# The first projection's weight split and the last value sum change place at the start of attention

## The chip, the cores and the metric

The kernel runs on one core of a Trainium2 chip. The metric is the device time of one execution in microseconds; a kernel's time is the median of its runs.

## What is computed

Two layers are applied to x (2048 x 1024, float32); each is an attention block and a spectral block with residuals:

```python
qkv = (lambda x, *d: x.transpose(*d))((x @ wqkv).reshape(B, S, 3, H, Dh), 2, 0, 3, 1, 4)
q, k, v = qkv[0], qkv[1], qkv[2]
scores = jnp.einsum("bhqd,bhkd->bhqk", q, k) * (Dh ** -0.5)
p = _softmax(scores, axis=-1)
o = jnp.einsum("bhqk,bhkd->bhqd", p, v)
return (lambda x, *d: x.transpose(*d))(o, 0, 2, 1, 3).reshape(B, S, D) @ wo
...
x = x + _A_ref(_layernorm(x, axis=-1), A_wqkv, A_wo)
x = x + _B_ref(_layernorm(x, axis=-1), B_w_r, B_w_i)
x = x + _A_ref(_layernorm(x, axis=-1), A_wqkv, A_wo)
x = x + _B_ref(_layernorm(x, axis=-1), B_w_r, B_w_i)
```

There are 32 heads of 32 columns. `_B_ref` multiplies the two-dimensional Fourier transform of its input by a weight and transforms back; the change does not touch it.

## The kernel before, in words

`attention` (called once per layer) handles the heads in 8 groups g of 4 heads, 128 columns each. Every float32 operand of a projection is split in a high and a low float16 half by `split` (ACT makes the high half, L167, VectorE the low one, L168); a projection is then three products: high by high, high by low, low by high.

**Weights.** `Weights.prep(ph)` is a generator for one phase ph: ("k", g), ("q", g) or ("v", g). It loads the weights in pieces of 256 KB from the SP queue (L251) into one of three staging buffers `wst`, then splits each piece into `wqk` (two buffers) or `wv`. In layer 0 it also takes the largest magnitude of each piece on VectorE (L259, tile `fw`).

**Projections.** `qk_chunk(ph, c)` makes 512 rows of keys or queries: 24 matmuls (L338) into one PSUM bank, then a split of the result and its square (L342). `v_tiles(ph, t)` makes one value sum, 256 rows for two groups: 48 matmuls (L382) into one bank, evacuated by two ACT instructions (L386). `bank()` gives these sums a bank: while the list `both` is not empty, o and x in turn; afterwards x alone, which exists once.

**Prologue.** The normalised input is written to `big` in float16 halves. Then the keys and queries of group 0 (four chunks each) and eight value sums are made, the latter as the list `vk`; three of them stand behind the loop over c, in bank o, x and o. Ahead of these three, `norms()` twice takes the largest squared norm of keys and of queries: matmuls with a matrix of ones (L355) and a maximum on VectorE (L357, `mqk`). `mkbias` makes the softmax bias from both on POOL: an all-reduce over the partitions (L363, `mall`) and three small instructions, the last at L368.

**Units.** After the prologue the order on TensorE and ACT is the order of the code, written by hand (`tc.manual_schedule`); the other engines are ordered by the scheduling layer. A unit is a group g, a chunk c of 512 queries and a tile kt of 128 keys. `S` makes its scores: 12 matmuls (L563) into two of the three double banks `psS`, then two exponentials on ACT (L567) into `p` (eight buffers). `PV` multiplies by the values (L573, bank o), two units at a time, at every even unit. `add` sums the exponentials on VectorE (L584 for the second unit of a chunk, L586 else). After every odd unit, the generator `filler` supplies eight matmuls of the next groups' projections: its first phase is ("k", 1), whose sums use bank x. It first calls `prep` for that phase, so the split stands behind the exponentials of the first two units.

The lines of the code in these steps are below; those numbers are the profile's.

Of the kernel before, what the change touches and what calls it, by code (L numbers as in the profile page):

```python
# [164 lines left out]
def split(nc, hi, lo, src, scale):  # L165

    nc.scalar.activation(hi, src, AF.Copy, scale=scale)  # L167
    nc.vector.scalar_tensor_tensor(lo, src, scale, hi, op0=ALU.mult, op1=ALU.subtract)  # L168


def run(g):
    for _ in g:
        pass
# [53 lines left out]
class Weights:  # L227
# [5 lines left out]
    def prep(self, ph):  # L233
        nc, ap, wp = self.nc, self.ap, self.wp
        kind, g = ph
        if kind == "v":
            w = self.W[ph] = ap.wvp.tile([128, 2, 8, 256], F16, name="wv")
            sl = [(w[:, 0, 4 * j:4 * j + 4, 128 * i:128 * i + 128], w[:, 1, 4 * j:4 * j + 4, 128 * i:128 * i + 128],
                   wp[g + i, 2, :, 512 * j:512 * j + 512]) for i in range(2) for j in range(2)]
        else:  # L240
            w = self.W[ph] = ap.wqp.tile([128, 2, 8, 128], F16, name="wqk")
            sl = [(w[:, 0, 4 * j:4 * j + 4], w[:, 1, 4 * j:4 * j + 4],
                   wp[g, 0 if kind == "q" else 1, :, 512 * j:512 * j + 512]) for j in range(2)]
        st = []

        def load():
            if len(st) < len(sl):
                pool, tag = ap.stages[self.n % len(ap.stages)] if self.flag is not None and ph in PH0 else (ap.sgp, "wst")
                self.n += 1
                s = pool.tile([128, 4, 128], F32, name="wst", tag=tag)  # L250
                nc.sync.dma_start(s, sl[len(st)][2].rearrange("p (d c) -> p d c", c=128))  # L251
                st.append(s)
        for _ in range(4 if self.flag is not None and ph in PH0 else 3):
            load()
        yield
        for i, (h, l, _) in enumerate(sl):
            split(nc, h, l, st[i], SW)
            if self.flag is not None:
                nc.vector.tensor_reduce(self.flag.pop(), st[i], axis=AX.XY, op=ALU.max, apply_absolute_value=True)  # L259
            load()  # L260
            yield
# [6 lines left out]
def attention(nc, tc, layer, ap, xin, yd, wts, wo, cst, dram, flags):  # L268
# [4 lines left out]
    W, prep = wts.W, wts.prep  # L273
# [50 lines left out]
    def qk_chunk(ph, c):  # L324
        kind, g = ph
        w = W[ph]
        if c == 0:
            if kind == "k":
                K[g] = ap.k[g % 3]
            else:  # L330
                Q[g] = qp.tile([128, 2, 2048], F16, name="Q") if g % 2 else ap.q
            p_, n_ = (qp, "Q") if ph == ("q", 0) else (sq, "sq")
            nrm[ph] = p_.tile([128, 4, 512], BF16, name="sq", tag=n_)
        t = (K if kind == "k" else Q)[g][:, :, c * 512:c * 512 + 512]
        ps = bank()
        for d in range(8):
            for i, (a, b) in enumerate(((w[:, 0, d], xh[c][:, d]), (w[:, 0, d], xl[c][:, d]), (w[:, 1, d], xh[c][:, d]))):
                nc.tensor.matmul(ps, a, b, start=d == 0 and i == 0, stop=d == 7 and i == 2)  # L338
                if d < 7 or i < 2:
                    yield  # L340
        split(nc, t[:, 0], t[:, 1], ps, SQ / (SX * SW))
        (nc.gpsimd if both else nc.vector).tensor_tensor(nrm[ph][:, c], t[:, 0], t[:, 0], op=ALU.mult)  # L342
        if c == 3:
            left_norms.append(ph)
        yield
# [24 lines left out]
    def v_tiles(ph, t2):  # L370

        _, g = ph
        w = W[ph]
        if t2 == 0:
            V[g], V[g + 1] = ap.v[g % 3], ap.v[(g + 1) % 3]
        ps = bank().rearrange("p (t n) -> p t n", n=256)
        for j in range(2):
            c, o = t2 // 2, (t2 % 2) * 256 + j * 128
            for d in range(8):
                a, b = xh[c][:, d, o:o + 128], xl[c][:, d, o:o + 128]  # L380
                for i, (l, r) in enumerate(((a, w[:, 0, d]), (a, w[:, 1, d]), (b, w[:, 0, d]))):
                    nc.tensor.matmul(ps[:, j], l, r, start=d == 0 and i == 0, stop=d == 7 and i == 2)  # L382
                    if (3 * d + i) % 2 and (j, d, i) != (1, 7, 2):
                        yield
        for i in range(2):
            nc.scalar.activation(V[g + i][:, 2 * t2:2 * t2 + 2], ps[:, :, 128 * i:128 * i + 128], AF.Copy, scale=1.0 / (SX * SW))  # L386
        yield
# [4 lines left out]
    phases = [ph for g in range(NG - 1) for ph in beside[g]]  # L392

    def sums(ph):
        return 8 if ph[0] == "v" else 4

    def filler():
        run(prep(phases[0]))
        for i, ph in enumerate(phases):
            nxt = prep(phases[i + 1]) if i + 1 < len(phases) else iter(())  # L400
            for n in range(sums(ph)):
                yield from (v_tiles if ph[0] == "v" else qk_chunk)(ph, n)
                for _ in range(1 + (n > 0)):
                    next(nxt, None)
            run(nxt)
# [95 lines left out]
    def wo_rest(t):  # L501
        p = psS.tile([128, 2, 512], F32, name="s")
        nc.vector.bn_aggr(mvs[:, 2 * t:2 * t + 2], wo_last(t // 4, t % 4, p, wo_dst[t], wo_dst[t], True))
# [19 lines left out]
    vk = [v_tiles(PH0[0], t) for t in range(8)]  # L523
# [16 lines left out]
    for c in range(NCH):  # L540
        for i, ph in enumerate(PH0[1:]):
            if c < 2:
                ln(8 + 4 * c + 2 * i, 2)
            run(qk_chunk(ph, c))
        if c == 3:
            norms()
            norms()
        else:
            run(vk.pop(0))
    for v in vk:  # L550
        run(v)
    both.clear()
# [4 lines left out]
    def S(g, c, kt):  # L557

        s = [psS.tile([128, 2, 512], F32, name="s") for _ in range(2)]
        for i, (a, b) in enumerate(((0, 0), (0, 1), (1, 0))):  # L560
            for h in range(4):
                r = slice(32 * h, 32 * h + 32)
                nc.tensor.matmul(s[h // 2][:, h % 2], K[g][r, a, kt * 128:kt * 128 + 128],  # L563
                                 Q[g][r, b, c * 512:c * 512 + 512], start=i == 0, stop=i == 2)
        for hf in range(2):
            p = P[g, c, kt, hf] = pp.tile([128, 2, 512], F32, name="p")
            nc.scalar.activation(p, s[hf], AF.Exp, bias=bias[g], scale=SCALE / (SQ * SQ))  # L567
# [65 lines left out]
    with tc.manual_schedule(engines={mybir.EngineType.PE, mybir.EngineType.Activation}):  # L633
        for g in range(NG):
            todo = sum(sums(ph) for ph in beside.get(g, []))
            sl = slots(fill, todo, 22 if g == NG - 2 else 32, 24)
            wsl = slots(wof, 4, 10, 21)
            for u in range(NCH * NKT):
                c, kt = divmod(u, NKT)
                S(g, c, kt)  # L640
                if kt % 2 == 0:
                    for w in pend:
                        PV(*w)
                    late = pend
                    pend = []
                for w in late[:1]:
                    add(*w)
                    if w[2] == NKT - 1:
                        fin(*w[:2])
                        done = [w[:2]]  # L650
                late = late[1:]
                if kt == 5 and done:
                    out(*done.pop())
                pend.append((g, c, kt))
                if kt % 2 == 0:
                    continue
                if todo:
                    todo = next(sl)
                elif g == NG - 2:
                    if left:  # L660
                        run(lwo)
                        left = 0
                    if next(wsl, None) is not None and u == NCH * NKT - 1:
                        run(wsl)
                elif g == NG - 1:
                    for _ in range(share[u // 2]):
                        next(wof)
                    if u // 2 in rests:
                        wo_rest(rests[u // 2])
                if g == NG - 2 and todo < 4:  # L670
                    for _ in range(2):
                        if left > (8 if todo == 3 else 0):
                            next(lwo, None)
                            left -= 1
        for w in pend:
            PV(*w)
        for w in late + pend:
            add(*w)
        run(wof)
# [559 lines left out]
```

## Time and profile before

| what | value |
|---|---|
| median of 3 runs | 3857.41 us (3855.62 to 3857.58) |
| profiled execution | 3855.25 us |
| its span, first to last instruction | 3853.3 us |
| instructions in the span | 79584 |
| PE busy | 3720.5 us (97%) |
| DVE (VectorE) busy | 3165.8 us (82%) |
| ACT (ScalarE) busy | 2898.3 us (75%) |
| POOL (GpSimd) busy | 303.0 us (8%) |
| mean granted TensorE clock | 0.990 |

PE is the matmul side of TensorE, PEld its weight loads, SPq the queue from which SyncE issues DMAs. A row of the timeline gives the start in microseconds from the span's start, the length, the engine, the line, the operation, written tile <- read tiles, the shape and how many instructions were merged into the row; in brackets stands how long the engine was idle before and what ended that. "Granted clock" is the share of full TensorE clock that the chip allowed in a stretch.

### The profile page before, as it was taken

The numbers are of one execution on the slowest core, as the hardware profiler recorded it, in microseconds if no ns is written. First come the engines' busy times: TensorE is split into PE (matmuls) and PEld (weight loads), VectorE is DVE, ScalarE is ACT, GpSimd is POOL, SyncE is SP. The second block draws the span as 40 slices with busy tenths as digits, with TensorE's granted clock in tenths as the row PEclk, the third lists the DMA queues.
The fourth block names the chain that finished last, engine by engine and source line by source line (L and its number), as shares of the span: only waits on it lengthen the run. The fifth ranks groups of instructions, "written<-read, shape, count | busy, mean of one in ns | idle before, by whom it ended". The sixth has DMA issues, their size and how long they took to land.

```text
span 3853.3 us, 79584 instructions
## 1 busy us (share of the span) xinstructions
PE 3720.5 (97%) x32951; PEld 1640.1 (43%) x32951; DVE 3165.8 (82%) x3869; ACT 2898.3 (75%) x3567; POOL 303.0 (8%) x386
## 2 busy tenths in 40 slices
PE   6999999999999999999989999999999999999998
PEld 4322433342234233378853334333423432333788
DVE  6699899889998988866666998899899889889554
ACT  4678887888788866667756888888888888666585
POOL 1000000000000000004320000000000000000143
PEclk9999999999999999999999999999999999999999
DMA  8000000000000221243270000000000002112433
GB/s 206 15 12 23 12 12 18 18 12 18 12 26 7 73 71 64 80 149 124 63 175 15 18 18 13 12 18 23 10 18 12 23 12 91 53 64 72 150 99 104
DMA packets 165573, 194.07 MB, mean 50 GB/s; under 512 B 74960, under 2 KB 120656, under 8 KB 164176
## 3 DMA queue, kind: packets, MB, share of 16 engines
q1 hardware_dynamic: 164912, 188.82, 15.9%
q8 instruction: 260, 4.26, 0.5%
q14 instruction: 113, 0.93, 0.1%
q10 hardware_dynamic: 288, 0.07, 0.0%
HBM read 123.83 MB, written 48.23 MB: 45 GB/s over the span
## 4 chain that ended last, share of the span: by engine, by line
PE 73%; DVE 12%; issue 8%; ACT 3%; DMA 2%; POOL 2%; SPq 0%; DVEq 0%; POOLq 0%; ACTq 0%
PE o L573 19%; PE s L563 16%; PE x L338 12%; PE x L382 7%; PE x L441 6%; DVE R L586 4%; PE s L441 2%; PE ps L861 2%; PE ps L801 2%; ACT p L567 1%; PE s L592 1%; PE ps L792 1%; DMA wst<-in_wp 1%; PE ps L976 1%; PE ps L930 1%
## 5 line engine op out<-in xcount | busy, mean ns | idle before, releaser
L567 ACT ACTIVATE p<-s,bias 128x1024 f32<-128x1024 f32 x2048 | 2167.8, 1111 | 553.5 <-PE s L563 542.6
L586 DVE TENSOR_TENSOR R<-R,p 128x1024 f32<-128x1024 f32 x1792 | 2085.4, 1219 | 111.2 <-ACT p L567 107.8
L573 PE MATMUL o<-p,R 128*32 128x512 f32 x8192 | 985.0, 598 | 0.0
L338 PE MATMUL x<-big,wqk 128*128 128x512 f16 x2880 | 682.7, 383 | 21.1 <-DVE Q L168 6.5
L563 PEld LDWEIGHTS <-R 32*128 32x128 f16 x12288 | 231.6, 92 | 760.3 <-issue 644.6
L338 PEld LDWEIGHTS <-wqk 128*128 128x128 f16 x3072 | 277.6, 98 | 458.5 <-issue 165.4
L563 PE MATMUL s<-R 32*128 32x512 f16 x6144 | 430.9, 378 | 10.6 <-ACT p L567 8.9
L573 PEld LDWEIGHTS o<-p,R 128*32 128x32 f32 x8192 | 213.7, 109 | 523.8 <-issue 523.8
L563 PE MATMUL s<-Q,R 32*128 32x512 f16 x6144 | 425.4, 378 | 7.5 <-DVE R L482 5.5
L382 PEld LDWEIGHTS <-big 128*128 128x128 f16 x3072 | 293.1, 99 | 144.3 <-issue 66.2
L382 PE MATMUL x<-wv,big 128*128 128x256 f16 x2688 | 320.5, 275 | 35.0 <-DMA big<-hl 35.0
L584 DVE SCALAR_TENSOR_TENSOR R<-p 128x1024 f32<-128x1024 f32 x128 | 153.8, 1203 | 198.9 <-ACT p L567 198.6
L441 PE MATMUL x<-big 128*128 128x512 f16 x1050 | 241.6, 380 | 0.0
L363 POOL PARTITION_ALL_REDUCE mall<-mqk x16 | 41.8, 2612 | 2325.5 <-DVE mqk L357 2313.9
L441 PEld LDWEIGHTS <-big 128*128 128x128 f16 x1344 | 124.3, 98 | 180.5 <-issue 42.7
L909 DVE TENSOR_TENSOR H<-G,H 128x512 f16<-128x512 f32 (+1 forms) x68 | 46.3, 680 | 113.1 <-ACT H L908 112.9
L861 PE MATMUL ps<-cbi,H 128*128 128x256 f16 (+1 forms) x792 | 100.5, 275 | 7.9 <-ACT H L908 6.2
L854 ACT COPY U<-ps 64x256 f32<-64x256 f32 (+1 forms) x272 | 97.0, 357 | 11.6 <-PE ps L861 6.4
L854 ACT COPY B<-ps 64x256 f32<-64x256 f32 (+1 forms) x272 | 97.0, 356 | 7.0 <-PE ps L861 2.8
L861 PE MATMUL ps<-cb,big 128*128 128x256 f16 x780 | 97.6, 275 | 0.0
L167 ACT ACTIVATE R<-x 128x512 f16<-128x512 f32 x88 | 52.6, 598 | 54.8 <-PE x L338 54.7
L806 DVE TENSOR_TENSOR big<-ps,big 128x512 f16<-128x512 f32 x64 | 44.4, 694 | 50.4 <-ACT big L805 50.3
(428 smaller groups left out, 2967.7 us busy)
## 6 DMA issues: line engine op xcount, KB each, us to landing
wst<-in_wp SPq DMA_DIRECT2D x96, 256.0 KB, 3.0
R<-y SPq DMA_DIRECT2D x32, 512.0 KB, 5.4
w<-in_w SPq DMA_DIRECT2D x60, 256.0 KB, 2.7
od<-ohl SPq DMA_DIRECT2D x56, 256.0 KB, 2.4
big<-od SPq DMA_DIRECT2D x16, 896.0 KB, 7.0
y<-R SPq DMA_DIRECT2D x20, 512.0 KB, 2.6
R<-in_x SPq DMA_DIRECT2D x16, 512.0 KB, 5.6
wst<-in_wo SPq DMA_DIRECT2D x32, 256.0 KB, 3.0
```

Of the source, the lines that this page charges most:

```text
L167: nc.scalar.activation(hi, src, AF.Copy, scale=scale)
L338: nc.tensor.matmul(ps, a, b, start=d == 0 and i == 0, stop=d == 7 and i == 2)
L382: nc.tensor.matmul(ps[:, j], l, r, start=d == 0 and i == 0, stop=d == 7 and i == 2)
L441: nc.tensor.matmul(p, a, b, start=start and d == ds[0] and i == 0, stop=stop and d == ds[-1] and i == 2)
L563: nc.tensor.matmul(s[h // 2][:, h % 2], K[g][r, a, kt * 128:kt * 128 + 128], Q[g][r, b, c * 512:c * 512 + 512], start=i == 0, stop=i == 2)
L567: nc.scalar.activation(p, s[hf], AF.Exp, bias=bias[g], scale=SCALE / (SQ * SQ))
L573: nc.tensor.matmul(O[g, c][32 * h:32 * h + 32], V[g][:, kt, 32 * h:32 * h + 32], P[g, c, kt, h // 2][:, h % 2], start=kt == 0, stop=kt == ...
L584: nc.vector.scalar_tensor_tensor(acc[hf], P[g, c, 0, hf], 1e-34, p, op0=ALU.add, op1=ALU.add)
L586: nc.vector.tensor_add(acc[hf], acc[hf], p)
L801: nc.tensor.matmul(pa[:, j], tt[:, j], mm[:, g], start=True, stop=True)
L854: nc.scalar.copy(ov[64 * r:64 * r + 64, a0:a0 + m, x], tl[64 * x:64 * x + 64, :m, r])
L861: nc.tensor.matmul(out, l, r, start=k == 0, stop=k == len(mm_) - 1)
```

## The change

```diff
@@ -395,7 +395,6 @@
         return 8 if ph[0] == "v" else 4
 
     def filler():
-        run(prep(phases[0]))
         for i, ph in enumerate(phases):
             nxt = prep(phases[i + 1]) if i + 1 < len(phases) else iter(())
             for n in range(sums(ph)):
@@ -547,6 +546,8 @@
             norms()
         else:
             run(vk.pop(0))
+    run(prep(phases[0]))
+    last_v = vk.pop()
     for v in vk:
         run(v)
     both.clear()
@@ -638,6 +639,8 @@
             for u in range(NCH * NKT):
                 c, kt = divmod(u, NKT)
                 S(g, c, kt)
+                if g == u == 0:
+                    run(last_v)
                 if kt % 2 == 0:
                     for w in pend:
                         PV(*w)
```

`phases[0]` is ("k", 1). Its preparation is moved from the start of `filler` to a place ahead of the last three value sums. The last of the eight value sums is taken out of the list and run between the scores of unit 0 and those of unit 1; `both` is empty by then, so it takes bank x. Both layers are changed alike. Between the second and the third piece of the diff lines count one higher in the changed kernel (L563 is L564 there, L567 is L568).

In the orders below the first place is ScalarE in layer 0, from the evacuation of the last key chunk to the first units. `R<-o 128x512` and `R<-x 128x512` are the high halves of key and query chunks, `R<-o 128x256` and `R<-x 128x256` evacuations of value sums, `p<-s,bias` the exponentials, `wqk<-wst` the split's high halves. Before:

```order
L167 ACTIVATE R<-o 128x512
L167 ACTIVATE R<-x 128x512
L386 ACTIVATE R<-o 128x256 x2
L386 ACTIVATE R<-x 128x256 x2
L386 ACTIVATE R<-o 128x256 x2
L567 ACTIVATE p<-s,bias 128x1024 x4
L167 ACTIVATE wqk<-wst 128x512 x2
L567 ACTIVATE p<-s,bias 128x1024 x8
```

And in the changed kernel:

```order
L167 ACTIVATE R<-o 128x512
L167 ACTIVATE wqk<-wst 128x512 x2
L167 ACTIVATE R<-x 128x512
L386 ACTIVATE R<-o 128x256 x2
L386 ACTIVATE R<-x 128x256 x2
L568 ACTIVATE p<-s,bias 128x1024 x2
L386 ACTIVATE R<-x 128x256 x2
L568 ACTIVATE p<-s,bias 128x1024 x10
```

The two high halves moved from behind the fourth exponential to ahead of the last query chunk, and the last value sum's evacuation from ahead of the first exponential to behind the second.

The second place is VectorE in layer 0 at the same point. `wqk<-wst,wqk` are the split's low halves, `fw<-wst` the magnitudes of staged weights, `mqk<-s` the maxima for the bias, `R<-p` and `R<-R,p` the sums of exponentials. Before:

```order
L168 SCALAR_TENSOR_TENSOR R<-o,R 128x512 x2
L357 TENSOR_REDUCE mqk<-s 128x1
L168 SCALAR_TENSOR_TENSOR R<-x,R 128x512
L357 TENSOR_REDUCE mqk<-s 128x1
L584 SCALAR_TENSOR_TENSOR R<-p 128x1024 x2
L168 SCALAR_TENSOR_TENSOR wqk<-wst,wqk 128x512 x2
L259 TENSOR_REDUCE fw<-wst 128x1 x2
L586 TENSOR_TENSOR R<-R,p 128x1024 x8
```

And in the changed kernel:

```order
L168 SCALAR_TENSOR_TENSOR R<-o,R 128x512 x2
L168 SCALAR_TENSOR_TENSOR wqk<-wst,wqk 128x512 x2
L259 TENSOR_REDUCE fw<-wst 128x1 x2
L357 TENSOR_REDUCE mqk<-s 128x1
L168 SCALAR_TENSOR_TENSOR R<-x,R 128x512
L357 TENSOR_REDUCE mqk<-s 128x1
L585 SCALAR_TENSOR_TENSOR R<-p 128x1024 x2
L587 TENSOR_TENSOR R<-R,p 128x1024 x8
```

The low halves and two magnitudes moved ahead of both maxima. In layer 1 the low halves move in the same way, and there are no magnitudes. The two magnitudes belong to pieces that are loaded into the staging buffers which the split has freed.

The third place is TensorE in layer 0, where the second of the three late value sums (bank x) ends. Before, the third sum (bank o) follows it directly:

```order
L382 MATMUL x<-wv,big 128x256
L382 LDWEIGHTS big
L382 MATMUL x<-wv,big 128x256
L382 LDWEIGHTS big
L382 MATMUL o<-wv,big 128x256
```

In the changed kernel unit 0's twelve score matmuls follow it, and where these end stand:

```order
L564 LDWEIGHTS R
L564 MATMUL s<-R 128x512
L382 LDWEIGHTS big
L382 MATMUL x<-wv,big 128x256
L382 LDWEIGHTS big
```

The last sum's 48 matmuls moved behind unit 0's scores and into bank x. They are followed by unit 1's scores and the first eight matmuls of ("k", 1). POOL and the SP queue keep their order.

## The prediction, made before the result was known

> **What bounds the kernel now.** The first view is the chain of work that ended last, by engine:
>
> ```profile
> PE 73%; DVE 12%; issue 8%; ACT 3%; DMA 2%; POOL 2%; SPq 0%; DVEq 0%; POOLq 0%; ACTq 0%
> ```
>
> TensorE holds most of that chain, so the question at any place is when TensorE stands still. The change touches one place in each of the two layers: the passage from the prologue's value sums to the first score units. The second view is therefore the table by stretches (columns: length, busy time of PE, weight loads, DVE, ACT and POOL, then the granted TensorE clock), cut at that passage:
>
> ```profile
> 118.25:123.59 5.34, 5.34 (x50) 4.61 (x48) 0.00 (x0) 0.66 (x2) 1.05 (x3) 1.00 0.00 0
> 123.59:133.09 9.50, 5.18 (x33) 1.39 (x32) 3.56 (x4) 5.82 (x8) 0.00 (x0) 0.82 0.14 45
> 133.09:143.51 10.42, 10.42 (x98) 3.13 (x98) 8.94 (x9) 8.03 (x8) 0.00 (x0) 1.00 0.03 11
> 2046.81:2057.96 11.15, 6.95 (x46) 1.70 (x45) 3.57 (x4) 5.82 (x8) 0.00 (x0) 0.69 0.15 47
> ```
>
> During the last value sum (118.25 to 123.59) TensorE is busy throughout at clock 1.00. In the 9.50 us behind it, it works 5.18 us at a granted clock of 0.82, then it is full again. Layer 1 shows the same passage as 11.15 us, with 6.95 us of work at 0.69. The third view, the timeline, says what stands in it (layer 0, one engine's group per row: start, length):
>
> ```profile
> 113.67 0.37 POOL L363 PARTITION_ALL_REDUCE mall<-mqk  x1 [5.61 <-issue]
> 118.25 5.40 PE L382 MATMUL o<-wv,big 128*128 128x256 f16 x48
> 118.45 0.66 ACT L386 ACTIVATE R<-x 128x256 f32<-128x256 f32 x2 [4.58 <-PE x L382]
> 121.81 0.27 POOL L368 TENSOR_SCALAR bias<-bpr 128x1 f32<-128x1 f32 x1
> 123.59 1.03 PE L563 MATMUL s<-R 32*128 32x512 f16 x14
> 124.50 4.13 ACT L567 ACTIVATE p<-s,bias 128x1024 f32<-128x1024 f32 x4
> 125.67 0.82 PE L563 MATMUL s<-R 32*128 32x512 f16 x10 [1.04 <-ACT p L567]
> 127.66 2.36 DVE L584 SCALAR_TENSOR_TENSOR R<-p 128x1024 f32<-128x1024 f32 x2 [18.44 <-ACT p L567]
> 128.50 1.16 ACT L167 ACTIVATE wqk<-wst 128x512 f16<-128x512 f32 x2
> 129.94 1.29 DVE L168 SCALAR_TENSOR_TENSOR wqk<-wst,wqk 128x512 f16<-128x512 f32 x2
> 130.65 0.93 SPq L251 DMA_DIRECT2D wst<-in_wp  x2
> 130.68 2.49 PE L338 MATMUL x<-big,wqk 128*128 128x512 f16 x6 [0.56 <-DVE wqk L168]
> 133.10 0.82 PE L563 MATMUL s<-R 32*128 32x512 f16 x12
> 133.42 1.33 DVE L259 TENSOR_REDUCE fw<-wst 128x1 f32<-128x512 f32 x2 [2.20 <-DMA wst<-in_wp]
> 133.85 1.92 PE L573 MATMUL o<-p,R 128*32 128x512 f32 x16
> 133.96 2.12 ACT L567 ACTIVATE p<-s,bias 128x1024 f32<-128x1024 f32 x2 [4.29 <-PE s L563]
> ```
>
> Read it as a relay. Scores of unit 0 at 123.59; unit 1's second half has no free score bank (three banks, two per unit) until the first exponential ends, so it starts at 125.67. ACT makes four exponentials, 124.50 to 128.63, and only then rounds the weights of the first projection (128.50, x2). VectorE makes their low halves at 129.94. TensorE's eight projection matmuls wait for both: two begin behind the high half, six at 130.68. Unit 2's scores come at 133.10, its first exponential at 133.96. The bias that every exponential needs was ready at 121.81 + 0.27 = 122.08, so today it delays nothing.
>
> **The change, part by part.** No instruction is added or removed; in each layer 48 matmuls, 4 ACT and 2 or 4 VectorE instructions change place, and the last sum takes bank x instead of o.
>
> *The split moved ahead.* It now stands behind the evacuation of the last key sum, since it overwrites the buffer of the key weights. The rows around its new place:
>
> ```profile
> 101.17 0.60 ACT L167 ACTIVATE R<-o 128x512 f16<-128x512 f32 x1 [4.52 <-PE o L338]
> 101.80 0.69 DVE L168 SCALAR_TENSOR_TENSOR R<-o,R 128x512 f16<-128x512 f32 x1 [9.73 <-ACT R L167]
> 101.84 1.04 POOL L342 TENSOR_TENSOR sq<-R 128x512 bf16<-128x512 f16 x1 [9.38 <-ACT R L167]
> 106.77 0.69 DVE L357 TENSOR_REDUCE mqk<-s 128x1 f32<-128x512 f32 x1 [4.28 <-PE s L355]
> 107.38 0.68 DVE L168 SCALAR_TENSOR_TENSOR R<-x,R 128x512 f16<-128x512 f32 x1
> 108.53 0.69 DVE L357 TENSOR_REDUCE mqk<-s 128x1 f32<-128x512 f32 x1 [0.47 <-PE s L355]
> ```
>
> ACT rounds from 101.77 to 102.93 (2 x 0.58 from 1.16); its next duty is the query sum whose low half follows at 107.38, so it is hidden. VectorE makes the low halves from about 102.5 to 103.8 (1.29), also in idle time. In layer 0 two reductions of the *next* staged weights follow on VectorE, ahead of the two maxima from which the bias is made. They wait for DMAs that the freed stage buffers release. Before, the issue at 130.65 let the reduction run at 133.42, 2.77 us later. The first low half now ends at 103.15, so the reductions run from about 105.97 to 107.3 (1.33 for both). The first maximum then starts at 107.3 instead of 106.77, the other sum's low half at 108.0, the second maximum at 108.7 instead of 108.53: at most 0.17 us on the bias, 122.25 at worst. The all-reduce row starts 4.4 us behind that maximum's end, so perhaps nothing; I take 122.14 for the first exponential and keep 122.3 for the range. Layer 1 has no such reductions; its maxima don't move. The SP queue keeps its order: only those two weight DMAs go out earlier, about 103.2 and 103.8.
>
> [...]
>
> *The last value sum between units 0 and 1, layer 0.* How close groups follow each other is read in the steady loop:
>
> ```profile
> 152.09 1.90 PE L338 MATMUL x<-big,wqk 128*128 128x512 f16 x8
> 152.19 2.12 ACT L567 ACTIVATE p<-s,bias 128x1024 f32<-128x1024 f32 x2 [0.49 <-PE s L563]
> 153.92 0.82 PE L563 MATMUL s<-R 32*128 32x512 f16 x12
> 154.67 1.92 PE L573 MATMUL o<-p,R 128*32 128x512 f32 x16
> 154.78 2.12 ACT L567 ACTIVATE p<-s,bias 128x1024 f32<-128x1024 f32 x2 [0.47 <-PE s L563]
> ```
>
> Eight projection matmuls to the next scores take 153.92 - 152.09 = 1.83 us; scores to what follows 0.75; the exponential starts 0.86 behind its scores. Then:
> - Unit 0's scores start at 118.36 (when the last sum did, plus the 0.11 seen at 123.59). Their exponentials start at 122.14 and take 4.13 / 2 = 2.07: 124.21.
> - The last sum starts behind them and behind the evacuation of bank x (118.45 + 0.66 = 119.11): about 119.2, for 5.23, to 124.45. So TensorE works while the bias is made; that is the cover.
> - ACT evacuates it from 124.68 (0.2 behind the next group's start, as at 118.45) to 125.34; it is free by then.
> - Unit 1's scores: 124.48 to 125.23. Their banks are free since the first exponential's end, 123.2.
> - The projection's eight matmuls need bank x, thus 125.34: start 125.40. Weights and low halves lie ready since 104.
> - Unit 2's scores: 125.40 + 1.83 = 127.23; exponential 128.09. Unit 1's end at 127.5, so nothing waits.
>
> Against 133.96 this is **5.87 us** earlier. What goes is the wait for the bank, the wait for the weights and the half-speed matmuls (six in 2.49 us against eight in 1.90).
>
> *Layer 1*, where the bias is late relative to TensorE:
>
> ```profile
> 2037.22 0.37 POOL L363 PARTITION_ALL_REDUCE mall<-mqk  x1 [5.94 <-issue]
> 2041.48 5.40 PE L382 MATMUL o<-wv,big 128*128 128x256 f16 x48
> 2045.53 0.27 POOL L368 TENSOR_SCALAR bias<-bpr 128x1 f32<-128x1 f32 x1
> 2056.57 1.46 PE L563 MATMUL s<-R 32*128 32x512 f16 x12
> 2057.96 1.92 PE L573 MATMUL o<-p,R 128*32 128x512 f32 x16
> 2058.07 2.12 ACT L567 ACTIVATE p<-s,bias 128x1024 f32<-128x1024 f32 x2 [5.18 <-PE s L563]
> ```
>
> Unit 0's scores at 2041.59; last sum 2042.42 to 2047.65. Bias 2045.80, exponentials 2045.86 to 2047.93, the evacuation only then, to 2048.59; TensorE, through with unit 1's scores at 2048.45, waits 0.2 us. Projection 2048.65, unit 2's scores 2050.48, exponential 2051.34. Against 2058.07: **6.73 us** earlier. It is more than in layer 0 because the cold stretch was longer (unit 2's twelve score matmuls took 1.46 against 0.82).
>
> Everything behind unit 2 stands in its old order on every engine and hangs on work of the kernel itself, so I carry both shifts to the end: 5.87 + 6.73 = 12.6 us. The profiled execution took 3855.25 (span 3853.3 and 1.95 around it), so it would take 3842.65. The three runs' median, 3857.41, lies 2.16 above it; on that scale the forecast is **3844.8 us**, -0.33%.
>
> **Rivals.**
>
> *The bias becomes the wait.* The all-reduce and three small POOL instructions took 113.67 to 122.08 = 8.41 and 2037.22 to 2045.80 = 8.58. Elsewhere they took longer:
>
> ```profile
> 383.80 4.64 POOL L363 PARTITION_ALL_REDUCE mall<-mqk  x1 [118.14 <-DVE mqk L357]
> 396.75 0.76 POOL L368 TENSOR_SCALAR bias<-bpr 128x1 f32<-128x1 f32 x1
> ```
>
> That is 383.80 to 397.51 = 13.71 us. With that length layer 0's bias comes at 127.38, exponentials 127.44 to 129.51, evacuation to 130.17, unit 2's scores at 132.06 instead of 133.10, or at about 133.7 if TensorE, idle since 125.2, gets matmuls at the 0.42 us of the 130.68 row (2.49 / 6). Layer 1: bias 2050.93, evacuation to 2053.72, then 1.83 + 0.75 at full clock or 8 x 0.42 + 1.46 cold, so the first value products stand at 2056.4 to 2058.6 against 2057.96. Both together gain between 2.6 and -1.2 us: 3855 to 3859, no change. For it: POOL's times do vary. Against it: both prologue rows are short, and VectorE was idle beside them, as it will be again until unit 1's first exponential ends (126.4; 2049.7), behind the bias. [...]
>
> *It doesn't do what it says.* If something unseen kept unit 0's scores behind the last sum (a score bank, a rounding of the queries), the split alone would help. The four exponentials would end at 128.63 as now, but the eight matmuls would follow unit 1's scores at 126.50: unit 2's at 128.33, not 133.10, with the bank wait of 1 us left. That is 4.77 us in layer 0; the same steps from 2046.81 put layer 1's exponential at 2052.4, 5.7 earlier; 10.5 together, 3846.9. The score banks were last read at 108.53 + 0.69, which speaks against it.
>
> *Slower: the loop falls into a worse step.* Group 0's 32 pairs of units run with ACT idle 0.49 + 0.47 us in a pair (152.19 and 154.78) and VectorE at 2 x 2.36 of 5.2 us. If starting with another spacing of exponentials and sums left VectorE behind, ACT would wait for the eight probability buffers in every pair. Place: group 0 of both layers, 64 pairs. It decides from 12.6 / 64 = 0.20 us a pair on; at 0.33 the loss is 21 - 12.6 = 8.5 us, 3866. Against it: ACT has 0.96 us to spare in a pair, and VectorE loses 1.29 + 1.33 us of duty at the loop's start, so it begins less behind than before.
>
> **How the numbers follow.** Forecast 0.80; the split alone works 0.06; the bias waits 0.08; the worse step 0.06. The forecast's own range: at best no bank wait in either layer (0.17 + 0.2 more) and an execution at the low end of the runs shown (1.8 under the median), 3842.6; I go to 3840.5 for the clock's phase, whose share I read only as 0.82 and 0.69. At worst the square's exclusion (0.3), the late bias (0.2) and, if the POOL instructions take the longer time in one layer alone, 5 us: 3850. The range 3840.5 to 3850 takes in the first two cases. Measurements of this kernel can tell about 0.2%, 7.7 us, from no change, so faster means under 3849.7: 0.86. Within it: 0.08. Slower: 0.06.
>
> **What would show it.** Right: in the rows of after, projection matmuls at about 125.4 with no gap before them, unit 2's exponential near 128.1 and 2051.3, granted clock 1.00 in the passage, unit 0's exponentials at 122.1 and 2045.9, and every later landmark shifted by 5.9, then 12.6. Wrong: an all-reduce that ends after 125 or 2048; maxima behind 109; a pair longer than 5.21; or a later stage that gives the shift back, such as a wait for a DMA whose issue did not move with it.

## The result, and the profile after

The changed kernel takes **3842.91 us** (median of 9 runs, 3839.59 to 3849.16), the kernel before 3857.41 (9 runs, 3851.55 to 3858.31): a ratio of 0.9966, 95% interval 0.9958 to 0.9975. That is 14.5 us less (9.6 to 16.2 by the interval) where 12.6 were forecast, 3842.91 against 3844.8.

The timeline of the changed kernel in layer 0, at the place that the prediction followed (start, length, engine, operation):

```profile
118.20 0.83 PE L564 MATMUL s<-R 32*128 32x512 f16 x12
119.02 5.40 PE L382 MATMUL x<-wv,big 128*128 128x256 f16 x48
121.81 0.27 POOL L368 TENSOR_SCALAR bias<-bpr 128x1 f32<-128x1 f32 x1
122.11 2.12 ACT L568 ACTIVATE p<-s,bias 128x1024 f32<-128x1024 f32 x2 [3.15 <-POOL bias L368]
124.35 0.83 PE L564 MATMUL s<-R 32*128 32x512 f16 x12
124.45 0.66 ACT L386 ACTIVATE R<-x 128x256 f32<-128x256 f32 x2 [0.22 <-PE x L382]
125.16 1.89 PE L338 MATMUL x<-big,wqk 128*128 128x512 f16 x8
125.21 2.12 ACT L568 ACTIVATE p<-s,bias 128x1024 f32<-128x1024 f32 x2
126.98 0.83 PE L564 MATMUL s<-R 32*128 32x512 f16 x12
127.84 2.12 ACT L568 ACTIVATE p<-s,bias 128x1024 f32<-128x1024 f32 x2 [0.51 <-PE s L564]
```

Unit 0's scores stand ahead of the last value sum, whose 48 matmuls cover the making of the bias; both exponentials of unit 0 wait for the bias alone (3.15 us, "POOL bias"). Unit 1's scores follow the sum, the projection matmuls follow them without a wait, and unit 2's first exponential is at 127.84 instead of 133.96. The table by stretches for the same passage in both layers (length, PE, weight loads, DVE, ACT and POOL busy, granted clock):

```profile
118.20:126.98 8.78, 8.78 (x81) 5.84 (x81) 0.62 (x1) 5.21 (x8) 1.05 (x3) 1.00 0.01 2
2039.03:2047.90 8.87, 8.80 (x82) 5.88 (x82) 0.71 (x1) 5.18 (x8) 1.05 (x3) 1.00 0.01 2
```

TensorE is busy throughout, 8.78 of 8.78 us in layer 0 and 8.80 of 8.87 in layer 1, and the clock that was 0.82 and 0.69 is 1.00. Layer 1, where the bias sets the pace a little:

```profile
2039.03 0.82 PE L564 MATMUL s<-R 32*128 32x512 f16 x12
2043.06 0.27 POOL L368 TENSOR_SCALAR bias<-bpr 128x1 f32<-128x1 f32 x1
2043.36 2.12 ACT L568 ACTIVATE p<-s,bias 128x1024 f32<-128x1024 f32 x2 [3.56 <-POOL bias L368]
2045.18 0.83 PE L564 MATMUL s<-R 32*128 32x512 f16 x12
2046.08 1.89 PE L338 MATMUL x<-big,wqk 128*128 128x512 f16 x8
2048.76 2.12 ACT L568 ACTIVATE p<-s,bias 128x1024 f32<-128x1024 f32 x2 [0.60 <-PE s L564]
```

To compare profiles, the execution is cut into pieces that every kernel here has: the **passage** from the start of the last but one value sum (bank x) to unit 2's first exponential, and the **middle** from there to the same sum of layer 1; the last column is what stands behind the passage of layer 1. All times in us, one profiled execution each, read from the timelines:

| kernel | passage, layer 0 | middle | passage, layer 1 | from there to the end |
|---|---|---|---|---|
| before | 20.95 | 1902.28 | 21.83 | 1795.23 |
| before, second profile | 21.41 | 1910.28 | 21.54 | 1792.57 |
| changed | 14.98 | 1905.86 | 15.06 | 1791.08 |
| changed, second profile | 15.02 | 1902.18 | 15.82 | 1793.65 |
| split alone | 16.10 | 1906.30 | 16.10 | 1793.96 |
| last value sum alone | 20.81 | 1902.51 | 19.85 | 1792.17 |
| layer 0 alone | 15.01 | 1901.78 | 21.84 | 1794.38 |
| layer 1 alone | 21.00 | 1903.21 | 15.46 | 1793.24 |
| changed, 8 more matmuls | 16.66 | 1900.33 | 14.98 | 1792.38 |
| changed, bank o | 14.90 | 1903.66 | 14.90 | 1794.65 |
| changed, late bias | 19.15 | 1906.17 | 19.17 | 1794.44 |
| changed, magnitudes of the high half | 14.98 | 1894.31 | 14.98 | 1796.27 |
| changed, no magnitudes | 15.16 | 1885.76 | 15.23 | 1791.36 |

The passages gained 5.97 and 6.77 us, 12.74 together. Between the two first profiles the middle lost 3.58 and the part behind the second passage gained 4.15; the experiments ask whether that belongs to the change.

### The profile page after: what moved, and what is told of

It reads as the page before. It is cut to its first block, busy times and chain, and to the rows that moved or that the text cites. A ratio compares the mean times of both kernels' runs of the same rounds, so it can differ in the third digit from the quotient of the medians.

```text
span 3839.8 us, 79585 instructions
## 1 busy us (share of the span) xinstructions
PE 3713.6 (97%) x32951; PEld 1637.3 (43%) x32951; DVE 3165.3 (82%) x3869; ACT 2900.6 (76%) x3567; POOL 309.1 (8%) x386
## 4 chain that ended last, share of the span: by engine, by line
PE 74%; DVE 11%; issue 8%; ACT 3%; DMA 2%; POOL 2%; SPq 0%; DVEq 0%; POOLq 0%; ACTq 0%
PE o L574 20%; PE s L564 17%; PE x L338 12%; PE x L382 7%; PE x L440 6%; DVE R L587 3%; PE s L440 2%; PE ps L864 2%; PE ps L804 2%; ACT p L568 1%; PE s L593 1%; PE ps L795 1%; PE ps L979 1%; DMA wst<-in_wp 1%; PE ps L933 1%
## 5 line engine op out<-in xcount | busy, mean ns | idle before, releaser
L568 ACT ACTIVATE p<-s,bias 128x1024 f32<-128x1024 f32 x2048 | 2169.8, 1112 | 553.6 <-PE s L564 536.7
L564 PEld LDWEIGHTS <-R 32*128 32x128 f16 x12288 | 231.2, 92 | 755.3 <-issue 639.8
L564 PE MATMUL s<-R 32*128 32x512 f16 x6144 | 430.2, 378 | 6.7 <-ACT p L568 5.0
L564 PE MATMUL s<-Q,R 32*128 32x512 f16 x6144 | 425.7, 378 | 7.1 <-DVE R L481 5.5
L382 PE MATMUL x<-wv,big 128*128 128x256 f16 x2784 | 331.9, 276 | 35.4 <-DMA big<-hl 35.4
L864 PEld LDWEIGHTS <-H 128*128 128x128 f16 (+1 forms) x792 | 76.6, 99 | 20.2 <-ACT H L911 7.1
```

Of the source, the lines that this page charges most:

```text
L864: nc.tensor.matmul(out, l, r, start=k == 0, stop=k == len(mm_) - 1)
```

## The experiments

The theory: TensorE stood still in the passage because of the order alone, and moving both pieces of work fills it; behind the passage nothing changes but chance. The rivals: one edit does it all; the bias has slack; time is given back in the middle because of the change. Each kernel was timed beside the kernel before on the same chip; "before" here is that median.

**The split alone.** The last value sum stays where it was.

```diff
     run(prep(phases[0]))
-    last_v = vk.pop()
...
-                if g == u == 0:
-                    run(last_v)
```

> Only the split is moved; the last value sum stays ahead of unit 0, in bank o. Theory: the wait for the weights was the larger part, so unit 2's first exponential comes near 129.2 in layer 0 (before 133.96, changed kernel 127.84) with a bank wait of about 1 us left between the two units, 4.8 us gained there and about 5.7 in layer 1; time 3844 to 3850, about 3847. Rival (both edits are needed): the four exponentials in a row still hold the eight matmuls back, unit 2 not ahead of 131, and the time stays above 3852.

3845.29 us against 3853.97 (ratio 0.9975, 0.9966 to 0.9985). Its timeline in layer 0:

```profile
124.40 4.13 ACT L567 ACTIVATE p<-s,bias 128x1024 f32<-128x1024 f32 x4
125.57 0.82 PE L563 MATMUL s<-R 32*128 32x512 f16 x10 [1.04 <-ACT p L567]
126.32 1.90 PE L338 MATMUL x<-big,wqk 128*128 128x512 f16 x8
129.02 2.12 ACT L567 ACTIVATE p<-s,bias 128x1024 f32<-128x1024 f32 x2 [0.48 <-PE s L563]
```

The four exponentials still stand in a row, but the projection follows unit 1's scores at once. What is left is the wait for the score bank, 1.04 us ahead of 125.57. The passage is 4.85 us shorter in layer 0 and 5.73 in layer 1, where 4.8 and 5.7 were expected: the wait for the weights was four fifths of the gain.

**The last value sum alone.** The split stays behind the first units' exponentials.

```diff
     def filler():
+        run(prep(phases[0]))
...
-    run(prep(phases[0]))
     last_v = vk.pop()
```

> Only the last value sum is moved between units 0 and 1, into bank x; the split stays behind unit 1's exponentials. Theory: the eight projection matmuls still wait for ACT's four exponentials, the rounding (about 128.5) and VectorE's low halves (about 130.0), so unit 2's first exponential comes at 132.1 to 132.8, only 1.2 to 1.9 us earlier, and 1.3 to 2.6 in layer 1; time 3852 to 3856. Rival (the covered bias is the gain): about half of the 14.5 us, 3850 or less.

3853.19 us against 3853.97 (0.9998, 0.9989 to 1.0007): no change that this measurement can tell. The timeline in layer 0:

```profile
122.64 2.12 ACT L568 ACTIVATE p<-s,bias 128x1024 f32<-128x1024 f32 x2 [4.10 <-POOL bias L368]
127.17 1.18 ACT L167 ACTIVATE wqk<-wst 128x512 f16<-128x512 f32 x2
128.62 1.28 DVE L168 SCALAR_TENSOR_TENSOR wqk<-wst,wqk 128x512 f16<-128x512 f32 x2
129.36 2.74 PE L338 MATMUL x<-big,wqk 128*128 128x512 f16 x6 [0.87 <-DVE wqk L168]
132.03 1.18 PE L564 MATMUL s<-R 32*128 32x512 f16 x12
133.25 2.12 ACT L568 ACTIVATE p<-s,bias 128x1024 f32<-128x1024 f32 x2 [4.90 <-PE s L564]
```

TensorE waits again for the rounding (127.17) and the low halves (128.62), and its matmuls are slow after the wait (six in 2.74 us). The passage gained 0.14 us in layer 0, less than the 1.2 expected, and 1.98 in layer 1. A late bias can account for most of what is missing in layer 0: in this profile unit 0's exponentials start 10.20 us behind the start of the last but one sum, 9.24 in the first profile of the changed kernel. So the two edits are not two halves: alone the second gave 0.14 and 1.98 us and its time cannot be told from before; behind the first it is worth 1.12 and 1.04, the wait for the score bank.

**One layer at a time.** The old order in the other layer.

```diff
     def filler():
+        if layer != 0:
+            run(prep(phases[0]))
...
-    run(prep(phases[0]))
-    last_v = vk.pop()
+    last_v = None
+    if layer == 0:
+        run(prep(phases[0]))
+        last_v = vk.pop()
...
-                if g == u == 0:
+                if g == u == 0 and last_v is not None:
```

> Both edits in layer 0 alone; layer 1 in the old order. Theory: layer 0's passage gives 5.9 to 6.1 us as in the changed kernel, layer 1's passage stays at its 11.1 us length between unit 0's scores and the first value products. Theory (phase): 0 to 4 us of it are given back at waits behind the passage that now meet a half-clock stretch (296.5 and 378.4), time 3851 to 3856. Rival (plain sum): nothing is given back, time 3850.5 to 3852.

3847.53 us against 3853.97 (0.9986, 0.9977 to 0.9995), 6.4 less. The time is below both ranges of the expectation, whose absolute times counted from 3857.41. Set against the kernel before beside it, the plain sum (5.9 to 6.1) fits, and a give-back of several us does not show in the median; the interval, 1.9 to 8.9 us less, does not exclude one. For layer 1 the condition is `layer == 1`:

> Both edits in layer 1 alone; layer 0 in the old order. Theory: layer 0 is as before to within 1 us, layer 1's passage (last value sum's old start to unit 2's first exponential) is 6.7 to 6.9 us shorter, and what else is gained or lost behind it is half-clock stretches met or missed; time 3846 to 3852. Rival (the two layers' gains hang together, for example through memory traffic between them): less than 4 us or more than 12.

3850.08 us against 3854.90 (0.9985, 0.9976 to 0.9994), 4.8 less; the passage is 6.4 us shorter than in the first profile of before, a little under the 6.7 expected; the bias was ready 10.02 us behind the start of the last but one sum there, 9.63 in the changed kernel's first profile. Layer 0's passage is 21.00 as before. The two medians' gains add up to 11.3, near what both layers give together.

**The same two kernels profiled again.** No edit.

> The changed kernel unaltered, profiled a second time. Theory (order): unit 2's first exponential again near 127.8 in layer 0, the passage of layer 1 again 6 to 7 us shorter than before, median near 3843. Theory (phase): the chip grants half clock in whole stretches of 3.41 us, and which of the later short waits of TensorE meets one depends on where the wait lies in the stretch. If the stretches keep the same place from execution to execution, the half-clock stretches stand again at 296.5 and 378.4 us and not at 57.7; if they don't, other waits are hit, and the spread of the times (3839.6 to 3849.2) is that lottery. Rival (queue): the 2 us lost at 293 to 300 come from VectorE being further behind, and then the wait there is 2.2 us in every profile, whatever the clock.

> The kernel before, profiled a second time. Theory (queue and stretch): the two passages take 20.9 and 21.8 us again within 1.5, and the stretch between them, 1902.28 us in the first profile and between 1900.3 and 1906.3 in the profiles of the other kernels, moves by some us though no instruction has changed. Rival (the change gives time back in the middle): the middle is again 1902.3 within 1, and its longer 1905.86 in the changed kernel belongs to the change.

The changed kernel took 3842.52 us beside 3853.97 (0.9975, 0.9965 to 0.9985), with passages of 15.02 and 15.82 us; the kernel before 3861.74 in its one run. In the table the middle of the *unchanged* code moves by 8 us from one profile to the next (1902.28 and 1910.28), and the changed kernel's second middle is 1902.18. The rival that the change gives time back in the middle falls. What moves is visible at one place in layer 0, where the third key sum of group 2 has to leave bank x to the fourth (these sums are made during group 0). Rows of VectorE and TensorE there, of before, of the changed kernel and of its second profile:

```profile
292.39 1.32 DVE L259 TENSOR_REDUCE fw<-wst 128x1 f32<-128x512 f32 x2 [1.45 <-DMA wst<-in_wp]
301.18 2.75 PE L338 MATMUL x<-big,wqk 128*128 128x512 f16 x12 [1.70 <-DVE R L168]
```

```profile
286.70 1.32 DVE L259 TENSOR_REDUCE fw<-wst 128x1 f32<-128x512 f32 x2 [1.96 <-DMA wst<-in_wp]
295.48 4.32 PE L338 MATMUL x<-big,wqk 128*128 128x512 f16 x12 [2.21 <-DVE R L168]
```

```profile
285.89 1.31 DVE L259 TENSOR_REDUCE fw<-wst 128x1 f32<-128x512 f32 x2 [0.80 <-DMA wst<-in_wp]
294.66 2.75 PE L338 MATMUL x<-big,wqk 128*128 128x512 f16 x12 [1.03 <-DVE R L168]
```

In each, a magnitude reduction (L259) waits at the head of VectorE's queue for a weight DMA: 1.45, 1.96 and 0.80 us. The sums of exponentials behind it fill VectorE without a gap, so the low half that frees bank x comes late by as much, and TensorE waits 1.70, 2.21 and 1.03: each time 0.23 to 0.25 more. The landing of that DMA is the chance: VectorE is ready for the reduction 2.84 us behind the issue of the DMA in all three (issued at 288.10, 281.90 and 282.25), and the data come 4.29, 4.80 and 3.64 us behind it. A second chance comes on top. The table by stretches, cut into pieces of 3.41 us, for the changed kernel and for its second profile:

```profile
293.08:296.50 3.42, 1.21 (x9) 0.58 (x6) 3.42 (x5) 2.12 (x2) 0.00 (x0) 1.00 0.01 2
296.50:299.91 3.41, 3.41 (x13) 1.05 (x14) 3.41 (x4) 0.00 (x0) 0.00 (x0) 0.50 0.00 0
```

```profile
293.87:297.29 3.42, 2.63 (x12) 1.07 (x11) 3.42 (x6) 1.92 (x2) 0.00 (x0) 1.00 0.00 0
297.29:300.70 3.41, 3.41 (x41) 0.86 (x40) 3.41 (x4) 2.12 (x2) 0.00 (x0) 1.00 0.02 5
```

A stretch with 1.21 of 3.42 us of matmul work was followed by a whole one at clock 0.50; one with 2.63 was not. So both the queue's and the stretches' theory hold a part. The wait makes the idle time, but it is not 2.2 us in every profile, as the queue's theory had it; and the stretches do not keep their place (a border at 296.50 in the first profile, at 297.29 in the second). In the second profile the wait was shorter, and also cut by the border of two stretches. An earlier wait of the changed kernel's first profile speaks for the border's counting by itself:

```profile
236.39 1.89 PE L338 MATMUL x<-big,wqk 128*128 128x512 f16 x8 [2.29 <-DVE Q L168]
```

It is longer than the 2.21 us before the half clock at 296.5, but a border at 235.06 (18 stretches of 3.413 us ahead of 296.50) cuts it in 0.96 and 1.33 us. The stretches on both sides of that border have 2.46 and 2.08 us of matmul work, and the matmuls behind the wait run at full clock (eight in 1.89 us, clock 1.00 from 231.64 to 241.88).

**Eight more matmuls.** A pad behind the last value sum in layer 0, whose product nothing reads.

```diff
                     run(last_v)
+                    if layer == 0:
+                        sp = psS.tile([128, 2, 512], F32, name="s")
+                        for _ in range(8):
+                            nc.tensor.matmul(sp[:, 0], xh[0][:, 0, 0:128], xh[0][:, 0], start=True, stop=True)
```

> The changed kernel with eight further matmuls (a product that nothing reads, 1.7 us at full clock) behind the last value sum in layer 0. Theory (phase): the pad shifts everything behind it by about 1.7 us against the clock's stretches of 3.41 us, so that the two waits at 293.3 to 295.5 and 375.1 to 377.1 no longer lie inside one stretch; if the stretches stand where they did, the half clock at 296.5 and 378.4 is gone, and by 390 us the padded kernel is level with or ahead of the changed one (-1.5 to +0.3 us), though 1.7 us of work were added. Rival (queue): the waits stay as slow as they were, and the padded kernel stays 1.7 us behind from the pad on.

3840.90 us against 3854.90 (0.9962, 0.9948 to 0.9976). The passage grew by 1.68 us as it should, and the middle was 1900.33, so the kernel was ahead of the first profile of the changed one. Of the two half-clock stretches the one at 296.5 us is gone, but one stands at 377.2. The DMA wait ahead of the first was itself shorter in this run (0.25 us), and the second profile without a pad reached 1902.18. The run cannot tell a shift against the stretches from a luckier landing: inconclusive.

**Bank o for the moved sum.**

```diff
     for v in vk:
         run(v)
-    both.clear()
...
                     run(last_v)
+                    both.clear()
```

> The changed kernel, but the last value sum between the units keeps bank o, so that the eight projection matmuls need not wait for its evacuation. Theory: TensorE's small gap ahead of those matmuls goes (0.06 us in layer 0, 0.15 in layer 1), unit 2's first exponential at most 0.2 us earlier; time the same as the changed kernel's to within its spread. Rival (the bank is a bottleneck of the new order): over 0.5 us earlier in each layer.

3844.08 us against 3854.90 (0.9970, 0.9958 to 0.9982); passages 14.90 and 14.90, 0.08 and 0.16 shorter. Bank x is no bottleneck of the new order.

**A late bias.** Five idle POOL instructions in group 0's bias.

```diff
         nc.gpsimd.tensor_tensor(b, b, cst["half"], op=ALU.pow)
+        for _ in range(5 if g == 0 else 0):
+            nc.gpsimd.tensor_tensor(b, b, cst["ones"][:, 0:1], op=ALU.pow)
```

> The changed kernel with five further POOL instructions (a power with exponent 1, about 0.70 us each) in group 0's bias, so that the bias comes about 3.5 us later in both layers. Theory: unit 0's exponentials were ahead of the last sum's evacuation by only 0.2 us in layer 0 and behind it by 0.1 in layer 1, so the passage grows by 3.2 to 3.5 us in each layer (14.98 and 15.06 to about 18.3 and 18.5), by up to 2.5 more where TensorE's idle time brings a half-clock stretch; time 3848 to 3853. Rival (the bias has slack behind the last sum): less than 1 us in each passage, time as the changed kernel's.

3851.96 us against 3856.78 (0.9988, 0.9979 to 0.9997): more than half of the gain is gone. The timeline in layer 0:

```profile
125.97 0.27 POOL L370 TENSOR_SCALAR bias<-bpr 128x1 f32<-128x1 f32 x1
126.27 2.12 ACT L570 ACTIVATE p<-s,bias 128x1024 f32<-128x1024 f32 x2 [6.68 <-POOL bias L370]
127.44 1.37 PE L566 MATMUL s<-R 32*128 32x512 f16 x10 [2.08 <-ACT p L570]
128.99 2.86 PE L338 MATMUL x<-big,wqk 128*128 128x512 f16 x8 [0.19 <-ACT R L388]
```

The bias comes 3.5 us later in relation to the value sums, and the passages grow by 4.17 and 4.11: the delay, and slow matmuls behind the wait (eight in 2.86 instead of 1.89). The longest wait appears at unit 1's scores, which need the bank that the first exponential frees; what holds the projection is the evacuation of bank x behind unit 0's exponentials. The second profile of the changed kernel shows the same without any edit, in layer 1:

```profile
2040.79 0.27 POOL L368 TENSOR_SCALAR bias<-bpr 128x1 f32<-128x1 f32 x1
2043.81 1.89 PE L338 MATMUL x<-big,wqk 128*128 128x512 f16 x8 [0.73 <-ACT R L386]
```

There the bias was ready 10.38 us behind the start of the last but one sum instead of 9.63, TensorE waited 0.73, and the passage was 15.82 instead of 15.06. The rival of the late bias was a real mechanism; the POOL instructions were just quick enough.

**The magnitudes taken from the high half.** If VectorE waits for DMAs only because a reduction stands at the head of its queue, let it read what the split has made.

```diff
-                nc.vector.tensor_reduce(self.flag.pop(), st[i], axis=AX.XY, op=ALU.max, apply_absolute_value=True)
+                nc.vector.tensor_reduce(self.flag.pop(), st[i] if ph in PH0 else h, axis=AX.XY, op=ALU.max, apply_absolute_value=True)
...
+    nc.vector.tensor_scalar(flags["w"][:, 16:56], flags["w"][:, 16:56], 1.0 / SW, None, op0=ALU.mult)
     nc.vector.reduce_max(fw, flags["w"], axis=AX.X)
```

> The changed kernel, but the magnitudes of the weights behind the prologue are taken from the split's high half instead of the staged piece (scaled back once at the end), so that VectorE no longer waits for a weight DMA at the head of its queue. Theory (queue): VectorE's waits for those DMAs (16.7 us in 15 places before) go, with them most of TensorE's waits of 1.5 to 2.5 us in layer 0's groups, and the middle between the passages falls by 5 to 13 us; time 3830 to 3838. Rival (stretches alone): TensorE's waits stay, the middle is within 1900 to 1906 and the time is the changed kernel's.

**3827.24 us** against 3856.78 (0.9922, 0.9908 to 0.9935): it beats both kernels, and it lies below the expected range. Its middle is 1894.31, 6.0 to 11.9 less than the other kernels with both edits. Who waited for whom between 134 and 1150 us (us in total, times, longest), of the changed kernel's first profile and of this one:

```profile
DVE fw L259 <- DMA wst<-in_wp: 7.8, 10, 2.3
PE x L338 <- DVE Q L168: 5.7, 3, 2.3
PE x L338 <- DVE R L168: 3.2, 3, 2.2
```

```profile
PE x L338 <- DVE Q L168: 3.7, 3, 1.2
```

VectorE's wait for the weight DMA is gone, and with it part of TensorE's. So is half clock: none stands between 37 and 1658 us, where the changed kernel's first profile has it at 78.1, 296.5 and 378.4 (granted clock over the span: 0.993 here, 0.992 there). The prologue gained too: the passage of layer 0 begins at 108.13 instead of 112.87, which was not expected. In the changed kernel (and in the kernel before, with a wait of 4.36 us) the same chain stands there once more, and longer:

```profile
77.34 0.69 DVE L259 TENSOR_REDUCE fw<-wst 128x1 f32<-128x512 f32 x1 [4.49 <-DMA wst<-in_wp]
77.94 0.68 DVE L168 SCALAR_TENSOR_TENSOR R<-x,R 128x512 f16<-128x512 f32 x1
78.68 3.68 PE L338 MATMUL x<-big,wqk 128*128 128x512 f16 x10 [4.35 <-DVE R L168]
```

A reduction waits 4.49 us for its piece, the low half of a sum waits behind it, and TensorE 4.35 us for that bank.

**No magnitudes.**

```diff
-            if self.flag is not None:
+            if self.flag is not None and ph not in PH0:
+                nc.vector.memset(self.flag.pop(), 0.5)
+            elif self.flag is not None:
```

> The changed kernel without the magnitudes of the weight pieces behind the prologue in layer 0; a constant stands in their place, so that this part of the input check is left out. Theory (queue): as with the high halves, the waits of TensorE in layer 0's groups go; the middle falls by 5 to 14 us, at most 3 us more than there, for the 0.67 us reductions saved. Rival: the waits stay because something else than the reductions puts VectorE behind; middle 1900 to 1906.

3817.75 us in one run, against a median of 3856.78 beside it; middle 1885.76, 8.6 below the kernel with the high halves, where at most 3 was expected. TensorE's waits for VectorE at the bank changes, 5.7 and 3.2 us in the table above, no longer appear among the waits between 134 and 1150 us; the longest that is left is that for the squares (who waited for whom, as above):

```profile
PE s L357 <- DVE sq L344: 2.2, 3, 0.7
```

So the reductions seem to cost more than their waits: where VectorE is full, their own 0.67 us each would push the low halves back too. This rests on one run of the kernel without them.

## Why the prediction was right

It was right in sign, size and cause. By its steps:

- **The split's new place.** Forecast: rounding hidden, maxima at 107.3 and 108.7. The timeline of after:

```profile
101.69 1.04 POOL L342 TENSOR_TENSOR sq<-R 128x512 bf16<-128x512 f16 x1 [9.38 <-ACT R L167]
102.25 1.63 DVE L168 SCALAR_TENSOR_TENSOR wqk<-wst,wqk 128x512 f16<-128x512 f32 x2
106.14 1.44 DVE L259 TENSOR_REDUCE fw<-wst 128x1 f32<-128x512 f32 x2 [2.26 <-DMA wst<-in_wp]
107.49 0.68 DVE L357 TENSOR_REDUCE mqk<-s 128x1 f32<-128x512 f32 x1
108.69 0.68 DVE L357 TENSOR_REDUCE mqk<-s 128x1 f32<-128x512 f32 x1
```

The maxima stand at 107.49 and 108.69. The two low halves took 1.63 us, 1.29 before, 0.34 more: the first, which starts while POOL's square runs (101.69 to 102.73), took 1.03 us, the second 0.68. In layer 1, again beside a square, the two took 1.62. The worst end of the forecast's range counts 0.3 us for "the square's exclusion"; no run shows an exclusion, and in its place stand these 0.34 us, which never reached the bias. The all-reduce kept its distance to the square that precedes it on POOL (idle 5.61 before, 5.51 after; 5.47 to 5.92 in layer 0 of all profiles), while the second maximum ended 4.45 us ahead of it before and 4.05 after: there was slack behind the maxima.
- **Layer 0.** Forecast 5.87, measured 5.97 by the passage. The bias was ready at 122.08 as forecast, to the digit by luck: the all-reduce started 0.25 us earlier than before, and the bias took as much longer from there (8.66 us, 8.41 before). The projection started at 125.16, 0.24 ahead of the forecast, since the prologue was 0.15 earlier and the evacuation 0.1 sooner.
- **Layer 1.** Forecast 6.73, measured 6.77, with 0.15 us between unit 1's scores and the projection where 0.2 was forecast.
- **Both shifts carried to the end.** The passages together gave 12.74 where 12.60 was forecast. The step that this hangs on, that nothing behind the passage gives or takes, holds only on average: single profiles differ by 8 us in the middle with no edit at all. The first profiles' further 0.7 us (3.58 lost, 4.15 and, ahead of the passage, 0.15 gained) and the medians' further 1.8 lie inside that spread. The second set of the changed kernel gives 11.5 against the kernel before beside it, so nothing clear of the spread is left that needs a cause. That the median of after lies within 2 us of the forecast is then luck as well: the kernel before alone has medians from 3853.97 to 3857.41 in the sets of this document.
- **The rivals.** The late bias is the one that could have happened: it costs nearly one for one from the point where it decides (3.5 us later, passages 4.17 and 4.11 longer with the slow matmuls), and that point was nearer than the prediction had it. In layer 0 the evacuation waited only 0.22 us for the last sum once ACT was free (row 124.45), where the prediction's times leave 0.47; and the matmuls behind TensorE's wait were slow on top (eight in 2.86 us instead of 1.89), as the rival's second price had it. The split alone gave 4.85 and 5.73 where its rival had 4.77 and 5.7. The worse step of the loop did not come: undisturbed pairs of units are 5.2 us as before, and from unit 2's first exponential to the first scores of group 1 pass 178.0 and 174.9 us in the two profiles of the changed kernel, 176.0 and 180.1 in those of the kernel before.

## What to carry to other kernels

Where an engine waits at the seam between two phases and its order is that of the code, list what each of its next pieces waits for, move first the preparation that is the last to arrive, and then lay work that waits for nothing over the latency that remains; the second alone gave a time here that can't be told from before. A check or statistic that reads freshly loaded data must not stand at the head of a full engine's queue: read instead something that the engine has to wait for anyway (here the middle fell from 1905.86 and 1902.18 us to 1894.31). And before a gain or loss of a few microseconds far from an edit is explained, profile the same kernel twice.

## What the runs showed of the hardware that was not expected

Half clock came in whole stretches of 3.41 us, one, two or five in a row in the first profiles of both kernels (the last, at the end of the span, aside), and an idle time of about 2.2 us inside one stretch was enough (busy 1.21 of 3.42, then clock 0.50), while one with 2.26 us of work, in the kernel before, was followed by full clock:

```profile
300.03:303.44 3.41, 2.26 (x11) 1.06 (x11) 3.41 (x5) 1.60 (x2) 0.00 (x0) 1.00 0.01 2
303.44:306.85 3.41, 3.41 (x39) 0.86 (x40) 3.41 (x4) 2.12 (x2) 0.00 (x0) 1.00 0.02 5
```

In all 13 profiles, cut at the clock's own borders from 60 us on, a full-clock stretch with less than 1.49 us of matmul work was always followed by half clock and one with more than 1.77 us never; between them both occur. In the first profile of the kernel before, the highest work ahead of half clock is 1.33 us (3252.56 to 3255.97) and the lowest ahead of full clock 1.52 (238.59 to 242.00); in that of the changed kernel 1.51 was followed by half clock (375.01 to 378.42) and 1.50 by full (1986.10 to 1989.51). Where the stretches lie is not fixed to the program's start: the first half clock begins at 30.26 us in one profile of the changed kernel and at 31.05 in the other.
